# Taps two to a product on half-width tiles, state tiles and loads regrouped, and more of the scan's scaling on ScalarE, in a gated sum of an S5 scan and a long convolution

## The chip, the core and the metric

The kernel runs on one core of one Trainium2 chip. The metric is device time in microseconds (us) of one execution. The engines named below are TensorE (PE in the profile; PEld is its weight load), VectorE (DVE), ScalarE (ACT), GpSimd (POOL) and SyncE (SP). SyncE only hands out transfers (its queue is SPq); GpSimd hands out the transfers that add to their destination.

## What is computed

S = 2048 steps, D = 1024 channels, P = 1024 complex states, all inputs in bf16. The reference, cut:

```python
def A(x, Lambda, B, C, log_dt, Dskip):              # the scan
    Lam_bar = exp(exp(log_dt) * Lambda)
    Bu = x @ (((Lam_bar - 1) / Lambda)[:, None] * B).T
    h[t] = Lam_bar * h[t - 1] + Bu[t]
    return 2 * (h @ C.T).real + x * Dskip
def Bf(q, k, v, shift_k, ssm_k, ssm_D):             # the convolution, q is x
    k_shift[t] = sum(k[t - i] * shift_k[:, i] for i in range(4))    # the four taps
    kv = k_shift * v
    return q * (causal_conv(kv, ssm_k) + kv * ssm_D)
g = sigmoid((x * gate_w).sum(-1, keepdims=True))
out = g * A(...) + (1 - g) * Bf(x, k, v, ...)
```

## The kernel before

**Order.** The instructions of every engine are issued in the order of the program (`put`, line 92; nearly all instructions therefore have line 94 in the profile, and groups are told apart by their tiles). What decides is thus where a step is written, on its own engine's queue and on those of the engines it needs. Generators (`step`, `steps`, `run`, line 948) interleave the parts of longer jobs by hand.

**The convolution** runs over NC = 8 chunks of 128 channels. For a chunk: `load` (line 175) brings k transposed (kT), the filter transposed (kn) and v; `taps` (476) makes the four taps by products with diagonal matrices `dg` (`dgs`, 304); `times_v` (506) multiplies by v and splits into sum and difference (mirror); `fold_K`/`mirror_K` do the same with the filter; `fwd_K` (542) and `fwd_V` (565) transform by products with cosine and sine tables (tiles psk and psv); `products` (578) multiplies the spectra on VectorE; `inverse` (628) transforms back (tile psz) and stores to a scratch in DRAM (cv_scr). The loop from line 1004 is a pipeline: iteration c takes the products of chunk c, the inverse of chunk c-1, the transforms of chunk n = c+1, and the taps and fold of chunk nn = c+2. `tap_sums` (457) has, for each of 16 blocks of 128 steps, four products of a 128 x 128 piece of kT, moved by one step each, with a 128 x 128 diagonal: 64 products of 128 columns a chunk. kT, kn and the v of chunks 0 and 1 share a pool of three rooms (`ld`, 142); v of later chunks comes for two chunks at a time into a tile of the pool of x (`xt_pool`). A `held` load waits for a small write of ScalarE into its tile.

**The scan** has NTB = 4 blocks of 512 steps and NG = 4 groups of 256 states: 16 state tiles in the order of `order` (678), each made in two halves j by products of x and B (`Bu`, 693). Tiles 0 to 3 are made as even and odd steps apart (`Bu_tile`, 717; tiles odd and even), the later ones plain (`Bu_plain`, 743; tile both) and turned afterwards by ScalarE and an adding transfer (`turn_U`). The convolution's loop takes nine of the first twelve halves; three (b0, b1, b2) come after it, at line 1153. `scan` (777) is VectorE's: turn, scan, turn back (hb), and the even steps' share of the odd ones, through two scaled copies q, made by VectorE in scans 0 to 11 and by ScalarE in scans 12 to 14. `turn_C` (1117) scales C's columns: two products by ScalarE, two by VectorE, and a sum, by VectorE or, for 4 and 5, by an adding transfer. `plan` (1223) lists which halves (B), rows (C) and groups of rows (G) of the output products (tile psy) follow each scan.

## Time and profile before

| | us |
|---|---|
| three runs: median, lowest, highest | 399.96, 399.20, 402.22 |
| the profiled execution, and its span | 400.61, 398.8 |
| busy TensorE, VectorE, ScalarE, GpSimd | 386.1, 376.8, 287.4, 72.2 |
| 512 products of the taps, busy | 31.2 |
| 52 scalings q<-hb by VectorE, mean and busy | 0.355, 15.2 |
| 12 scalings Q<-hb by ScalarE, mean and busy | 0.709, 7.7 |
| 6 sums CT<-CT,m by VectorE, mean | 1.226 |

A row of the groups gives the operation, output <- input by the program's names, the number of instructions, busy time (overlaps counted once), the mean duration of one, and the idle time of the engine ahead of them with what ended it. Durations of matmuls include their way through the array, so that a stream of them advances faster than the mean suggests: a stream's time divided by its number is the pace. The chain of waits is the work that ended last, followed back from the end.

### The profile page before, as it was taken

The numbers are of one execution on the slowest core, as the hardware profiler recorded it, in microseconds if no ns is written. First come the engines' busy times: TensorE is split into PE (matmuls) and PEld (weight loads), VectorE is DVE, ScalarE is ACT, GpSimd is POOL, SyncE is SP. The second block draws the span as 40 slices with busy tenths as digits, with TensorE's granted clock in tenths as the row PEclk, the third lists the DMA queues.
The fourth block names the chain that finished last, engine by engine and source line by source line (L and its number), as shares of the span: only waits on it lengthen the run. The fifth ranks groups of instructions, "written<-read, shape, count | busy, mean of one in ns | idle before, by whom it ended". The sixth has DMA issues, their size and how long they took to land.

```text
span 398.8 us, 6544 instructions
## 1 busy us (share of the span) xinstructions
PE 386.1 (97%) x2437; PEld 206.0 (52%) x2437; DVE 376.8 (94%) x610; ACT 287.4 (72%) x434; POOL 72.2 (18%) x96
## 2 busy tenths in 40 slices
PE   8999899999999999999999999979999999999995
PEld 5456357474656647566444444424444444444442
DVE  8799999999999999999999899999999999999944
ACT  4797995969878796765429799936978874996201
POOL 3011030200202011020001010503344233433000
PEclk9999999999999999999999999989999999999999
DMA  7969993996929398097994799978999998988402
GB/s 160 159 142 223 205 261 70 231 213 138 210 58 230 56 156 190 28 156 113 209 204 88 180 196 188 195 164 167 199 188 178 253 261 142 218 163 170 121 0 106
DMA packets 129601, 65.72 MB, mean 165 GB/s; under 512 B 106393, under 2 KB 113313, under 8 KB 129570
## 3 DMA queue, kind: packets, MB, share of 16 engines
q1 hardware_dynamic: 117664, 42.22, 48.7%
q0 software_dynamic: 11824, 23.07, 33.8%
q8 instruction: 19, 0.31, 0.3%
q14 instruction: 12, 0.10, 0.1%
q10 hardware_dynamic: 82, 0.02, 0.0%
HBM read 12.86 MB, written 8.39 MB: 53 GB/s over the span
## 4 chain that ended last, share of the span: by engine, by line
PE 68%; DVE 19%; ACT 6%; issue 4%; DMA 2%; POOL 0%; DVEq 0%; ACTq 0%; POOLq 0%
PE psy L94 27%; PE both L94 12%; PE psk L94 7%; PE taps L94 5%; PE psz L94 4%; DVE BT L94 4%; PE psv L94 3%; PE foldk L94 3%; PE even L94 3%; DVE wkh L94 3%; DVE CT L94 2%; ACT Vh L94 2%; PE odd L94 2%; DVE W L94 2%; DMA ks<-lo 2%
## 5 line engine op out<-in xcount | busy, mean ns | idle before, releaser
L94 PEld LDWEIGHTS <-BT 128*128 128x128 bf16 x640 | 62.2, 98 | 47.8
L94 PE MATMUL both<-xT,BT 128*128 128x512 bf16 x384 | 83.7, 379 | 0.0
L94 PE MATMUL psy<-CT,hb 128*128 128x512 bf16 x256 | 59.4, 387 | 2.3 <-DVE CT L94 2.3
L94 PE MATMUL psy<-CT,U 128*128 128x512 bf16 x256 | 57.4, 379 | 0.0
L94 PEld LDWEIGHTS <-hb 128*128 128x128 bf16 x256 | 25.3, 99 | 33.9 <-issue 5.1
L94 POOL DMA_DIRECT2D U<-Q x24 | 23.3, 983 | 100.8 <-ACT Q L94 61.0
L94 ACT ACTIVATE U<-both 128x512 bf16<-128x512 f32 x48 | 26.4, 593 | 20.4 <-PE both L94 20.1
L94 PEld LDWEIGHTS <-U 128*128 128x128 bf16 x256 | 25.1, 98 | 30.2
L94 ACT ACTIVATE Vh<-psv 128x1024 bf16<-128x1024 f32 x32 | 31.0, 1033 | 11.9 <-PE psv L94 11.9
L94 DVE TENSOR_TENSOR_SCAN W<-rv,init,A 128x256 bf16<-128x256 f32 x48 | 32.2, 730 | 0.0
L94 PE MATMUL taps<-dg,kT 128*128 128x128 bf16 x512 | 31.2, 223 | 0.0
L94 POOL DMA_DIRECT2D G<-wkh x8 | 9.7, 1218 | 115.5 <-DVE wkh L94 115.5
L94 PEld LDWEIGHTS <-kT 128*128 128x128 bf16 x512 | 29.8, 100 | 1.0 <-issue 0.2
L94 PEld LDWEIGHTS <-SF 128*128 128x128 bf16 x184 | 18.0, 98 | 20.0 <-issue 1.5
L94 PE MATMUL psk<-eok,SF 128*128 128x512 bf16 (+1 forms) x120 | 28.1, 354 | 0.0
L94 ACT ACTIVATE Q<-U,lam 128x512 bf16<-128x512 bf16 (+1 forms) x48 | 27.7, 606 | 0.0
L94 PE MATMUL psz<-G,CI 128*128 128x512 bf16 x64 | 24.3, 380 | 2.4 <-DVE G L94 1.9
L94 PE MATMUL psz<-G,SI 128*128 128x512 bf16 x64 | 24.3, 379 | 0.0
L94 DVE TENSOR_TENSOR wkh<-BT,Vh 128x3072 bf16<-128x3072 bf16 (+4 forms) x20 | 21.8, 1111 | 0.0
L94 DVE TENSOR_TENSOR wkh<-Kh,Vh 128x3072 bf16<-128x3072 bf16 (+2 forms) x16 | 21.3, 1350 | 0.0
L94 ACT ACTIVATE BT<-psy,gcols 128x1024 bf16<-128x1024 f32 x5 | 5.4, 1109 | 21.8 <-PE psy L94 21.8
L94 ACT ACTIVATE m<-psy,gcols 128x1024 bf16<-128x1024 f32 x8 | 8.9, 1113 | 16.6 <-PE psy L94 16.6
(189 smaller groups left out, 780.7 us busy)
## 6 DMA issues: line engine op xcount, KB each, us to landing
U<-Q POOLq DMA_DIRECT2D x24, 256.0 KB, 5.3
G<-wkh POOLq DMA_DIRECT2D x6, 768.0 KB, 8.1
cv_scr<-cv SPq DMA_DIRECT2D x16, 256.0 KB, 2.6
v<-in_B_v_dram SPq DMA_DIRECT2D x3, 1024.0 KB, 9.6
out_dram<-m SPq DMA_DIRECT2D x8, 256.0 KB, 5.6
BT<-cv_scr SPq DMA_DIRECT2D x7, 256.0 KB
out_dram<-BT SPq DMA_DIRECT2D x7, 256.0 KB, 2.0
ks<-lo POOLq DMA_DIRECT2D x6, 256.0 KB, 7.4
```

The lines of the kernel that those rows point to most:

```text
L94: i = f(*a, **kw)
```

## The change

- **Taps.** Chunks 2 to 7 use a packed form. `spread` copies kT so that the partitions hold 64 channels twice, the second time moved by two steps: kB for the upper channels and kT itself for the lower ones. A product then makes two taps of 64 channels at once (`packed_sums`), with `dg` tiles of 128 x 64. There are still 64 products a chunk, of 64 columns. `columns` makes the coefficients for this with eight small products and two steps of VectorE.
- **Loads.** kB takes a room of `ld`; v is loaded for chunks 2 and 3 together and then one chunk at a time into halves of one tile. The loads of the next chunk stand right behind the taps, in the order v (held), B or x, kT, kn. The loads of x for block 2 stand at the head of iteration 6.
- **State tiles.** Tiles 0 to 3 are spread in smaller parts over iterations 1 to 6, three halves of tiles 4 and 5 are run in iteration 6, and one after the loop; b10 (the first half of tile 8) moves ahead of the scans, and tile 13 ahead of the first output row, in rooms of its own.
- **Scaling.** Scans 4, 5, 6, 9, 10 and 11 have q made by ScalarE, as 12 to 14 had. C's columns 0 and 1 are summed by adding transfers, and the turning of 6 and 7 stands inside scan 3.

```diff
-            w = 1 if c < 2 else 2
-            if w == 1:
-                t = ld.tile([128, NT, 1, 128], BF16, name="v", tag="ld")
+            w = 2 if c == 2 else 1
+            if c == 2:
+                lds["v2"] = xt_pool.tile([128, NT, 2, 128], BF16, name="v2", tag="xT")
+            if c < 2:
+                t = ld.tile([128, NT, 128], BF16, name="v", tag="ld")
             else:
-                t = xt_pool.tile([128, NT, 2, 128], BF16, name="v2", tag="xT")
-            move(t.rearrange("p n k d -> p n (k d)"),
-                 vf.rearrange("(n p) d -> p n d", p=128)[:, :, c * 128:(c + w) * 128])
+                t = lds["v2"][:, :, c % 2:c % 2 + w].rearrange("p n k d -> p n (k d)")
+            if held:
+                hold(t[:, 0, 0:1])
+            move(t, vf.rearrange("(n p) d -> p n d", p=128)[:, :, c * 128:(c + w) * 128])
             for k in range(w):
-                lds["v", c + k] = t[:, :, k]
+                lds["v", c + k] = t[:, :, k * 128:(k + 1) * 128]
             return
...
             load_t(t[:, PAD:], kf[:, cc])
+            if c >= 2:
+                lds["kB", c] = ld.tile([128, PAD + S], BF16, name="kB", tag="ld")
         lds[which, c] = t
+    def spread(c):
+        a, b = lds["kT", c], lds["kB", c]
+        lo, hi, n = slice(0, 64), slice(64, 128), PAD + S
+        move(b[lo, 8:], a[hi, 8:])
+        move(b[hi, 10:], a[hi, 8:n - 2])
+        yield
+        move(a[hi, 10:], a[lo, 8:n - 2])
     kT0 = ld.tile([128, PAD + S], BF16, name="kT", tag="ld")
-    v0 = ld.tile([128, NT, 1, 128], BF16, name="v", tag="ld")
+    v0 = ld.tile([128, NT, 128], BF16, name="v", tag="ld")
     put("pool", nc.gpsimd.memset, kT0[:, 0:PAD], 0.0)
...
         load_t(kT0[:, PAD + hs.start:PAD + hs.stop], kf[hs, 0:128])
-        move(v0[:, ns, 0], vf.rearrange("(n p) d -> p n d", p=128)[:, ns, 0:128])
-    lds["kT", 0], lds["v", 0] = kT0, v0[:, :, 0]
+        move(v0[:, ns], vf.rearrange("(n p) d -> p n d", p=128)[:, ns, 0:128])
+    lds["kT", 0], lds["v", 0] = kT0, v0
     load("kn", 0)
...
         copy(gwb, psp[:, 1, KS * ND:(KS + 1) * ND])
+        for q in range(4):
+            for t in range(2):
+                mm(psp[t * 64:t * 64 + 64, 1, 64 + q * ND:64 + (q + 1) * ND],
+                   skr[:, q // 2 * 64:q // 2 * 64 + 64, q % 2 + 2 * t], ident[32:32 + ND, 32:32 + ND], True, True)
+        copy(pcol2, psp[:, 1, 64:64 + 4 * ND].rearrange("p (i j) -> p i j", j=ND))
+        tt(ident2, ident[:, 0:64], ident[:, 64:128], ALU.add)
     def dgs(c, on_dve=False):
+        if c >= 2:
+            dg = ks_pool.tile([128, 2, 2, 64], BF16, name="dg2", bufs=1)
+            for q in range(4):
+                if on_dve:
+                    ts(dg[:, q // 2, q % 2], ident2, pcol2[:, q, c:c + 1], None, ALU.mult)
+                else:
+                    act(dg[:, q // 2, q % 2], ident2, func=ACT.Identity, scale=pcol2[:, q, c:c + 1])
+            return dg
         dg = ks_pool.tile([128, KS, 128], BF16, name="dg", bufs=1)
...
+    def packed_sums(halves, dg, h):
+        ps = ps2([128, 8, 128], "taps")
+        for n in range(8):
+            for e, k in enumerate(halves):
+                for m in range(2):
+                    k0 = PAD + (8 * h + n) * 128 - m
+                    mm(ps[:, n, e * 64:e * 64 + 64], k[:, k0:k0 + 128], dg[:, e, m], m == 0, m == 1)
+        return ps
     def of_blocks(ks, h):
...
     def taps(c, dg):
-        kT = lds.pop(("kT", c))
+        kT, kB = lds.pop(("kT", c)), lds.pop(("kB", c), None)
         ks = ks_pool.tile([128, 4, 4, 128], BF16, name="ks")
         for h in range(2):
-            act(of_blocks(ks, h), by_block(tap_sums(kT, dg, h)), func=ACT.Copy)
+            sums = tap_sums(kT, dg, h) if c < 2 else packed_sums((kT, kB), dg, h)
+            act(of_blocks(ks, h), by_block(sums), func=ACT.Copy)
         kss[c] = ks
...
         tb, g = order[i]
+        if i == 13:
+            V_ = s5p["v13"].tile([128, 2, 2, HB], BF16, name="V13")
+            O_ = lam_pool.tile([128, 2, 2, HB + 2], BF16, name="O13", tag="lamd")
+            Us[tb, g] = V_, O_[:, :, :, 2:]
+            turns_U[i] = turn_U(g, V_, O_)
+            return [Bu_plain(tb, g, V_, O_, j) for j in range(2)]
         if i in (10, 11):
...
             else:
-                home = uu[0 if i in (0, 1, 13, 14) else 1] if i < 6 or i in (13, 14) else s5p["uu"]
+                home = uu[0 if i in (0, 1, 14) else 1] if i < 6 or i == 14 else s5p["uu"]
                 U = home.tile(shape, BF16, name="U")
...
                     act(ends[:, tb % 2, g], U[:, 1, :, :, HB - 1], func=ACT.Copy)
-                if halved:
-                    yield
+                yield
         yield
...
     put_off = []
+    scaled_by_act = (4, 5, 6, 9, 10, 11, 12, 13, 14)
...
             tt(hb[:, 1], hb[:, 1], b[:, 0], ALU.add)
-            by_act = tb == NTB - 1 and not last
-            if by_act:
+            by_act = tb * NG + g in scaled_by_act
+            if tb * NG + g == 3:
+                run(turning[7])
+            if by_act and tb == NTB - 1:
                 q = [s5p["Q"].tile([128, 2, 2, HB], BF16, name="Q") for k in range(2)]
...
-    old = ahead = none
-    tiles = (b for i in range(6) for b in Bu(i))
+    old = none
+    parts = (None for i in range(4) for b in Bu(i) for _ in b)
+    tiles = (b for i in (4, 5) for b in Bu(i))
...
         if c == 0:
+            load("kT", 2)
             load("kn", 2)
-            load("kT", 2)
             load("v", 2)
             load_BT(0, 0)
-        if c == 0:
+            run(spread(2))
             p1 = products(0, 1)
...
             step(tv)
+            load("kT", 3)
             load("kn", 3)
-            load("kT", 3)
             load_BT(0, 1)
...
             continue
-        if c == 1:
-            load("v", 4)
+        if c == 6:
+            load_xT(2)
         tabs, back, prod = turn_table(c - 1) if c <= NG else none, inverse(c - 1), products(c)
+        apart = spread(nn) if nn < NC else none
         step(old)
         step(tabs)
+        step(apart)
         step(back)
...
         run(back)
+        run(apart)
         run(old)
-        if c == 2:
-            load("v", 6)
         if nn < NC:
             dg = dgs(nn)
-        bu = next(tiles) if c == 4 else ahead if c == 6 else none
-        step(bu)
+        if c % 2 == 0:
+            step(parts)
         fwd_K(n, (0, 1))
-        step(bu)
+        if c % 2 == 0:
+            step(parts)
         fwd_K(n, (2, 3))
         if c == 6:
-            load_xT(2, held=True)
             run(sp)
...
             taps(nn, dg)
+        if nn + 1 < NC:
+            load("v", nn + 1, True)
+            if c == 1:
+                load_BT(1, 0)
+            elif c in (2, 3):
+                load_xT(1, (3 - c,))
+            load("kT", nn + 1)
+            load("kn", nn + 1)
+            if c == 1:
+                load_BT(1, 1)
         step(prod)
...
             step(tv)
-        bu = [next(tiles) for _ in range({1: 1, 2: 1, 3: 1, 5: 1, 6: 3}.get(c, 0))] + [none, none]
+        if c < 6:
+            steps(parts, 2)
+        else:
+            run(next(tiles))
+        fwd_V(n, (0, 1))
+        if c < 6:
+            step(parts)
+            if c in (1, 3):
+                step(parts)
+        else:
+            run(next(tiles))
+        fwd_V(n, (2, 3))
         if c == 5:
-            bu[1] = ahead = next(tiles)
-        step(bu[0])
-        fwd_V(n, (0, 1))
-        if nn + 1 < NC:
-            load("kn", nn + 1, True)
-            load("kT", nn + 1)
-        if c in (1, 2):
-            load_BT(1, c - 1)
-        elif c in (3, 4):
-            load_xT(1, (c - 3,))
-        step(bu[0])
-        step(bu[1])
-        fwd_V(n, (2, 3))
-        if bu[1] is not ahead:
-            step(bu[1])
-        run(bu[2] if c == 6 else none)
-        if c == 2:
+            step(parts)
+        elif c == 6:
+            run(next(tiles))
+        if c == 1:
             lam_diag(1, lam_pool)
...
     def turn_C(pi):
-        by_sum = pi in (4, 5)
-        if by_sum:
+        by_sum = pi in (0, 1, 4, 5)
+        if pi in (4, 5):
             m = [s5p["Q"].tile([128, D], BF16, name="Q") for c in range(2)]
...
     load_CT(0)
-    load_CT(1)
     load_BT(2, 0)
     load_BT(2, 1)
-    load_CT(2)
     load_BT(3, 0)
     load_BT(3, 1)
+    load_CT(1)
+    load_CT(2)
     load_CT(3)
...
         steps(prod, 3)
-        b0, b1, b2 = tiles
-        run(b0)
+        run(next(tiles))
         run(back)
         gate(1)
-        run(b1)
+        gate(2)
         run(prod)
...
         run(turns_U[6])
-        run(b2)
-        gate(2)
         steps(turning[0], 2)
...
         run(b8)
+        steps(turning[1], 2)
+        run(b9)
+        b10, b11 = Bu(8)
+        run(b10)
         back = inverse(c)
...
         run(back)
-        run(b9)
-        steps(turning[1], 2)
     h3.close()
...
     s5p["io"] = pool("io", 2)
+    s5p["v13"] = pool("v13", 1)
...
     NS = NTB * NG
-    plan = ["B8", "B9 B10", "B11", "B12 C0", "C1", "C2", "C3 B13", "B14 B15", "G10", "G11", "G12 G13", "G20", "G21",
+    plan = ["B8", "B9 B10", "B11", "B12 B13 C0", "C1", "C2", "C3 B14", "B15", "G10", "G11", "G12 G13", "G20", "G21",
             "G22 G23", "", ""]
...
         yield
+        if j == 3:
+            run(turning[6])
...
                 combine(k)
-                if tl == 1 and put_off:
-                    put_off[-1][0]()
+    run(turning[0])
+    run(turning[1])
     step(scans[0])
...
             else:
-                (Bu_next if unit[0] == "B" else Cy_row)(int(unit[1:]))
-        if put_off and j != 13:
+                (Bu_next if unit[0] == "B" else Cy_row)(int(unit[1:]), *([[b11]] if unit == "B8" else []))
+        if put_off:
             put_off[-1][0]()
```

## What I expected

> **What bounds the kernel now.** The profiled run took 400.61 us with a span of 398.8, 1.8 outside it; the median of the three runs, 399.96, is 0.65 lower. I read the page's totals, the chain of waits, the timelines of SyncE and TensorE at the places of the edits, the DMA list, and windows for the clock.
>
> ```profile
> PE 386.1 (97%) x2437; PEld 206.0 (52%) x2437; DVE 376.8 (94%) x610; ACT 287.4 (72%) x434; POOL 72.2 (18%) x96
> ```
>
> TensorE and VectorE are both nearly full, so a saving on one alone is worth little. The chain says who leads where:
>
> ```profile
> 46.48 1.90 PE psz L94 x8
> ...
> 58.73 3.68 PE taps L94 x64
> ...
> 212.03 0.78 PE p L94 x32
> ...
> 311.15 82.92 PE psy L94 x384
> ```
>
> From 31 to 46 it is VectorE, from 46.5 (iteration c=1) to 137 mostly TensorE, from 142 to 172 VectorE (products), to 223 TensorE, to 266 VectorE (first scans, C turned), then TensorE to 394.09. Two more views decide: SyncE's queue and TensorE in c=0.
>
> ```profile
> 24.91 3.72 SPq L94 DMA_TRANSPOSE kT<-in_B_k_dram  x1
> 28.68 0.58 SPq L94 DMA_DIRECT2D v<-in_B_v_dram  x1
> 29.31 6.49 SPq L94 DMA_TRANSPOSE BT<-in_A_B_re_dram  x1
> 35.90 3.56 SPq L94 DMA_TRANSPOSE kn<-in_B_ssm_k_dram  x1
> ```
>
> ```profile
> 32.62 3.74 PE L94 MATMUL taps<-dg,kT 128*128 128x128 bf16 x64
> ...
> 44.76 0.22 PE L94 MATMUL foldk<-rows,refl 1*128 1x128 bf16 x1
> 46.48 0.39 PE L94 MATMUL psz<-G,CI 128*128 128x512 bf16 x1 [1.49 <-DVE G L94]
> ```
>
> SyncE hands over a transpose in about 2 us and is held while the DMA engines are full; chunk 2's taps ran at 32.6, when SyncE was still at BT. TensorE then had 1.5 us of air before 46.48.
>
> **The taps.** Chunks 2 to 7 keep 64 products each, at 64 columns instead of 128. Pairs of weight load and product stream at 6.91/32 = 216 ns for 512 columns, 1.75/16 = 109 for 256, 3.68/64 = 57.5 for 128, and 0.78/32 = 24.4 for the gate's one column. The step per column is about 0.41 ns, so 64 columns should take 31 ns (bounds 24.4 and 57.5). That saves 26.5 x 64 = 1.70 us a chunk: 8.5 us for chunks 3 to 7, whose taps come after 46.48, and 1.7 in c=0, used below.
>
> **The copies.** Each such chunk gets three copies of 256 KB inside the on-chip memory on SyncE's queue; the third waits for the first two, and the taps wait for the third. The nearest rows are other 256 KB moves of that queue.
>
> ```profile
> cv_scr<-cv SPq DMA_DIRECT2D x16, 256.0 KB, 2.6
> out_dram<-BT SPq DMA_DIRECT2D x7, 256.0 KB, 2.0
> ```
>
> In c=0 the copies stand behind BT, whose handing over ends at 35.8. The first two go out at 35.9 and 36.5, behind 512 KB of BT and beside a gather: at the 290 GB/s that the DMA view shows there, BT lasts to 38, the pair to about 40.5. The third is issued then and lands 2.0 to 2.6 later: 43 (41.5 to 45). Taps(2) waits from 32.5 to 43, and behind it on TensorE stand the rest of K's transform, V's and the fold: 36.20 to 44.98, 8.8 us. Then 43 + 2.0 + 8.8 = 53.8 in place of 46.48, +7.3. VectorE waits too: chunk 1's products need that V. The clock adds to it; elsewhere it fell after waits of 1.28 and 1.03 us:
>
> ```profile
> 266.00:268.00 2.00, 1.77 (x5) 0.56 0.02 6
> 268.00:270.00 2.00, 2.00 (x7) 0.59 0.00 0
> ```
>
> That is 4 us at 0.57, 1.7 us lost; the 1.5 us wait at 46.48 lost none. I take 0.9, so **+8.2** (5.8 to 11). The Trainium skill ("TensorE: Matmul & The Clock Gate", Part 1) has the clock halve after an idle window of about 3.4 us. By that rule all 1.7 would be paid, the sum 0.8 higher; the trace agrees on the drop (0.56), not on the idle time it takes.
>
> In c=1 the queue is kT 3 and kn 3 (both waiting for taps(2), whose room they take), BT, two of xT, then the copies: five transposes of 2 to 2.7 us from 46.4 on, a pair at about 58, the third landing near 65.5. TensorE needs 12.2 us from psz (46.48) to taps (58.73), so it arrives at 66.9: 1.5 us of air. In c=2 to 4 two transposes fewer leave about 4. Behind SyncE's wait for the pair stand cv's second store and v; a store later by 2 us still precedes the next use of its buffer. I charge **+0.7** (0 to 20, see rivals). The extra 0.79 MB a chunk meets a DMA share of 0.70 to 0.86 there; the gathers into G have over 10 us until used.
>
> **State tiles.** Two more of 16 products, about 3.46 us each, run before c=7, and after the first psy row (C0) two fewer remain (U13 is ahead of it): +6.9 ahead, -6.9 behind. From c=1 to c=4 TensorE has 92.8 us now (four times 15.6 + 3.7 of taps + 3.9 of tile) and 93.7 then, VectorE some 22.7 each: TensorE still leads. In c=5 and c=6 VectorE leads (products, 22.5 us each, and the overlap), and new waits at psz(5) and V of chunk 7 come to 3.1 us against 2.2 now: **+0.9**. xT 2 must land before tile 4: v's room is free when VectorE is done with chunk 7's v, 9 us ahead of it; no cost, 2 us if late.
>
> **C turned by gather; q by ScalarE.** On VectorE two sums of 1.23 us go (C 0 and 1), with them its wait of 1.5 us for m, and the turning of 6 and 7 moves ahead of scan 3's q and U (2.5 us). So VectorE, 8.1 late at chunk 5's products, ends C 7 at 266.1 + 8.1 - 2.3 - 1.5 - 2.5 = 267.9. TensorE reaches C0 at 257.56 + 8.2 - 8.5 + 6.9 + 0.9 = 265.1 and its last group at 270.3, after it. What C0 loses now goes:
>
> ```profile
> 264.18 1.02 PE L94 MATMUL psy<-CT,hb 128*128 128x512 bf16 x4 [1.28 <-DVE CT L94]
> 266.23 9.60 PE L94 MATMUL psy<-CT,hb 128*128 128x512 bf16 x36 [1.03 <-DVE CT L94]
> ```
>
> Arriving at 257.56, its 6.9 us would end at 264.5; it ended, with the lower clock, at 268.9: **-4.4** (0 to -4.4). Six scans' q: 24 x 0.285 = 6.8 us leave VectorE after C0, where TensorE leads: worth nothing by itself, cover for the rest. ScalarE gets 24 x 0.62 = 15 us there, 79 busy of the 104 us from 266 to 370 becoming 94. Eight small products and two VectorE steps at the start cost **+0.4** (0 to 0.8). The holds on ScalarE are 0.2 us each, behind evictions TensorE has finished; v by chunk moves the same bytes.
>
> Sum: +0.4 + 8.2 - 8.5 + 0.7 + 0.9 - 4.4 = **-2.7 us**, so 397.9 on the profiled run's scale, 397 on the median's. With the bounds of these terms, 392 to 401.
>
> **Rivals.**
> - The copies of chunk 2 cost nothing: they pass BT on the DMA engines, or land in time some other way. For: 0.53 MB is 2 us of transfer. Against: the queue's order, and a handing over that ends at 35.8. It gives 8.2 less: 389.
> - The copies are late in every chunk, the case on the slower side: two hops, each in full DMA traffic beside the gathers.
>
> ```profile
> ks<-lo POOLq DMA_DIRECT2D x6, 256.0 KB, 7.4
> ```
>
>   At 5.5 us a hop instead of 2.6 the third lands 5.8 late, less air of 1.5 in c=1 and 4 in the three others: 4.3 + 3 x 1.8 = 9.7, so 407. It decides from 5.2 us a hop on. For: the row above, and v's 9.6 us for 1 MB. Against: that row is an accumulating gather on another queue, while plain moves show 2.0 to 2.6.
> - The weight load, not the columns, sets a product's pace: each stays at 57.5 ns and 8.5 + 1.7 come back, 407. Against it, the gate loads 128x128 weights for every column at 24.4 ns. The Trainium skill (same page, "LDWEIGHTS") times a load by its 128 columns at 107 ns whatever follows, which speaks for this rival; the 24.4 ns of the trace does not agree with that as a pace.
> - ScalarE, 90% full after C0, delays evictions. For: every q waits for its scan in ScalarE's queue ahead of psy's evictions. Against: four product buffers cover 20 us of rows. Some 3 us: 400.
>
> **How the numbers follow.** 1% is 4 us, about what a measurement of this kernel can tell from no change. Forecast 42%, 397 with its own range 392 to 401, some 15 of the 42 below 396; free copies 25% (389); late copies 18% (407); weight pace 5% (407); ScalarE 10% (400). Faster by over 1%: 15 + 25 = 40%. Within: 27 + 10 = 37%. Slower: 23%. The range 388 to 405 takes in the forecast, the free copies, ScalarE and the near end of the late copies, and leaves out about 2 in 10.
>
> **What would show it.** Taps on dg2 near 2.0 us for 64; more says weights. TensorE idle before chunk 2's taps from 32.5 to about 43 with the third copy as releaser, psz at 54 to 55 instead of 46.48; a psz near 47 says free copies. Waits for kT before the taps of chunks 3 to 7 under 2 us; several of 2 or more say late copies. C0 without a wait for C, and 0.56 gone from the clock there. ScalarE waited for by psy would say the fourth rival. If VectorE leads in c=1 to c=4, my count of TensorE there is wrong.

## The result and the profile after

The changed kernel takes 432.71 us (median of four runs, 429.15 to 434.01); the kernel before took 399.88 beside it. The ratio is 1.080 with an interval of 1.072 to 1.088: 8% slower, where 397 us and a range up to 405 were forecast. The profiled execution is the fastest of the four, 429.15 us with a span of 427.3; positions below are its own. The ratios below are to the kernel before, run beside each kernel; they leave out executions more than 1.5% slower than the fastest of their kernel, so that a ratio can differ from the quotient of two medians.

The page of the changed kernel: busy time of each engine, the granted clock by slices, and the chain's shares by line.

```profile
PE 378.3 (89%) x2411; PEld 200.8 (47%) x2445; DVE 367.2 (86%) x586; ACT 300.8 (70%) x456; POOL 76.0 (18%) x100
...
PEclk9996699799998998999999999999999999999998
...
PE psy L94 22%; SPq L94 10%; DMA kT<-kT 8%; DMA kB<-kT 6%; PE both L94 4%; PE taps L94 4%; ACT Q L94 3%; PE psv L94 3%; DVE BT L94 3%; ACT Vh L94 3%; PE odd L94 3%; DVE wkh L94 2%; DMA ks<-lo 2%; PE even L94 2%; ACT m L94 2%
```

TensorE and VectorE are each less busy by 8 to 10 us, and both have lost their full span: 89% and 86% where 97% and 94% stood. They wait. ScalarE has 13 us more to do and GpSimd 4, neither near full by the page. New on the chain are the two hops of the copies, 14% of the span, and SyncE's queue (SPq), 10%; and the clock has dips in the first two fifths, where it had none. TensorE's waits say the same (total, times, longest):

```profile
PE taps L94 <- DMA kT<-kT: 28.1, 5, 11.9
PE psy L94 <- ACT U L94: 5.0, 2, 3.4
```

The chain of waits in order of time (start, length, what) shows the hops one behind the other, here of c=0, c=1 and c=2:

```profile
36.76 5.59 DMA kB<-kT
...
42.41 2.87 DMA kT<-kT
...
45.33 3.60 PE taps L94 x64
...
62.47 9.64 DMA kB<-kT
...
72.17 5.14 DMA kT<-kT
...
...
93.75 4.25 DMA kB<-kT
...
98.07 7.68 DMA kT<-kT
```

In c=3 they took 4.40 and 7.68 us. Where the wait was long the taps then ran at half the clock. Windows around the taps alone (start:end, length, TensorE's busy time and products, VectorE, ScalarE, granted clock, DMA share, GB/s), the first after a wait of 11.92 us, the second after one of 1.64:

```profile
45.30:49.00 3.70, 3.60 (x64) 0.00 (x0) 1.06 (x2) 0.50 0.00 0
...
105.80:107.90 2.10, 2.06 (x64) 0.00 (x0) 0.93 (x1) 1.00 0.67 120
```

The second is the narrow product at full clock: 2.06/64 = 32 ns, against 57.5 of before.

### The profile page after: what moved, and what is told of

The parts are those of the page before. It is cut to its first block, busy times and chain, and to the rows that moved or that the text cites. A ratio compares the mean times of both kernels' runs of the same rounds, so it can differ in the third digit from the quotient of the medians.

```text
span 427.3 us, 6555 instructions
## 1 busy us (share of the span) xinstructions
PE 378.3 (89%) x2411; PEld 200.8 (47%) x2445; DVE 367.2 (86%) x586; ACT 300.8 (70%) x456; POOL 76.0 (18%) x100
## 4 chain that ended last, share of the span: by engine, by line
PE 41%; DMA 18%; ACT 17%; SPq 10%; DVE 9%; issue 4%; ACTq 0%; DVEq 0%
PE psy L94 22%; SPq L94 10%; DMA kT<-kT 8%; DMA kB<-kT 6%; PE both L94 4%; PE taps L94 4%; ACT Q L94 3%; PE psv L94 3%; DVE BT L94 3%; ACT Vh L94 3%; PE odd L94 3%; DVE wkh L94 2%; DMA ks<-lo 2%; PE even L94 2%; ACT m L94 2%
## 5 line engine op out<-in xcount | busy, mean ns | idle before, releaser
L94 PE MATMUL psy<-CT,hb 128*128 128x512 bf16 x251 | 57.3, 379 | 5.3 <-ACT U L94 5.0
L94 PE MATMUL psy<-CT,U 128*128 128x512 bf16 x236 | 53.4, 379 | 0.2
L94 PE MATMUL taps<-dg,kT 128*128 128x64 bf16 (+1 forms) x320 | 25.1, 222 | 29.6 <-DMA kT<-kT 28.1
L94 ACT ACTIVATE Vh<-psv 128x1024 bf16<-128x1024 f32 x32 | 31.0, 1034 | 11.5 <-PE psv L94 11.4
L94 POOL DMA_DIRECT2D U<-Q x22 | 21.5, 993 | 92.1 <-ACT Q L94 58.8
L94 ACT ACTIVATE ks<-taps 128x1024 bf16<-128x1024 f32 x14 | 14.0, 1025 | 33.1 <-PE taps L94 33.1
L94 PEld LDWEIGHTS <-kT 128*128 128x128 bf16 x320 | 22.4, 110 | 31.0 <-DMA kT<-kT 23.2
L94 ACT ACTIVATE U<-both 128x512 bf16<-128x512 f32 x44 | 24.1, 594 | 15.7 <-PE both L94 15.4
L94 DVE TENSOR_TENSOR U<-U,q 128x512 bf16<-128x512 bf16 (+2 forms) x42 | 19.2, 484 | 8.7 <-ACT q L94 8.1
L94 ACT ACTIVATE Q<-U,lam 128x512 bf16<-128x512 bf16 (+1 forms) x44 | 25.4, 606 | 0.0
L94 DVE TENSOR_TENSOR G<-BT,Vh 128x4096 bf16<-128x4096 bf16 (+1 forms) x5 | 9.3, 1862 | 15.2 <-ACT Vh L94 15.2
```

Of the source, the lines that this page charges most:

```text
L94: i = f(*a, **kw)
```

## The experiments

The milestones below are read from TensorE's timeline: the starts of psz(0) to psz(6), of row C0, and the end of the last product, in us. psz(c) opens iteration c+1, so what c=1 costs lies between psz(0) and psz(1). The two last rows are the first two experiments.

| | psz(0) | psz(1) | psz(2) | psz(3) | psz(4) | psz(5) | psz(6) | C0 | end |
|---|---|---|---|---|---|---|---|---|---|
| before | 46.48 | 69.63 | 93.21 | 117.19 | 140.35 | 164.41 | 193.80 | 257.56 | 394.1 |
| after | 57.87 | 89.73 | 115.09 | 144.42 | 172.56 | 196.43 | 226.32 | 293.95 | 422.8 |
| no copies | 47.13 | 72.02 | 95.64 | 119.13 | 142.97 | 166.84 | 198.10 | 264.15 | 393.0 |
| full taps, no copies | 47.25 | 72.15 | 97.48 | 122.60 | 148.13 | 172.00 | 203.23 | 269.00 | 399.5 |

The theory to test: the third copy comes late, two hops behind each chunk's load, and with the lower clock behind that wait it is the whole loss of the convolution; ScalarE's added q is a second loss, behind it.

**What the copies cost.**

```diff
...
-                lds["kB", c] = ld.tile([128, PAD + S], BF16, name="kB", tag="ld")
+                kB = ld.tile([128, PAD + S], BF16, name="kB", tag="ld")
+                put("pool", nc.gpsimd.memset, kB[:, 0:PAD], 0.0)
...
-            sums = tap_sums(kT, dg, h) if c < 2 else packed_sums((kT, kB), dg, h)
+            sums = tap_sums(kT, dg, h) if c < 2 else packed_sums((kT, kT), dg, h)
...
-            run(spread(2))
...
-        apart = spread(nn) if nn < NC else none
...
-        step(apart)
...
-        run(apart)
```

> The changed kernel without the three copies of each chunk: kB is allocated as before but only its first 16 columns are set, and the packed taps of chunks 2 to 7 read kT for both halves, so the sums of those six chunks are not K's taps. All else is the changed kernel's. Theory 1 (the whole loss of the convolution is the wait for the third copy and the lower clock behind it): taps(2) starts near 32.5 us, no wait of TensorE ahead of taps over 2 us in any chunk, psz(6) at 185 to 191 us instead of 226, median 391 to 399 us. Rival 1 (the added bytes and v's 256-byte rows hold up the gathers, and VectorE with them): only the copies' share of 4.7 of 5.8 MB goes, v's small rows stay, 400 to 410. Rival 2 (the new order of loads, state tiles and products loses the time): over 420.

399.83 us, ratio to before 1.0037 (1.0003 to 1.0071). Without the copies all 33 us of the loss are gone. Of the rivals, the order of loads and tiles is out, and v's small rows cost little, if anything. By differences of the table's rows the copies cost 10.7 us in c=0, 7.0 in c=1, 1.7 in c=2, 5.8 in c=3, 4.3 in c=4 and nothing more in c=5: 29.6. But psz(6) came at 198, not at 185 to 191: without the copies, and so without K's true taps, the kernel only draws level with before. Its TensorE waits:

```profile
PE psz L94 <- DVE G L94: 5.0, 2, 3.0
PE psy L94 <- ACT U L94: 3.4, 1, 3.4
```

VectorE's G is now what psz waits for in the convolution, and U's evictions by ScalarE are what psy waits for behind it.

**What the narrow taps bring.** The same with before's four full-width products in every chunk (`sums = tap_sums(kT, dg, h)`, and dgs as before).

> The changed kernel with before's four full-width products a tap block in all eight chunks, no copies and kB only touched (the output is the reference's again). Against the run without copies this tells what the narrower products are worth by themselves. Theory 1: 57.5 instead of 31 ns for each of 64 products in six chunks, 10.2 us where TensorE leads throughout: psz(6) 7 to 10 us later than without copies, median 399 to 408. Rival (VectorE leads the convolution once the copies are gone): under 3 us between the two runs.

406.26 us, ratio 1.0167 (1.0133 to 1.0201). Against the run without copies, 6.4 us of the median and 5.1 at psz(6), where 10.2 were counted. By the rows of the table the saving arrives whole in c=2, c=3 and c=4 (1.7, 1.6 and 1.7 us) and not at all in c=0, c=1 and c=5. At psz(0) the shorter taps turn into a longer wait for VectorE's G (TensorE's timeline, first without copies, then with full taps):

```profile
47.13 0.45 PE L94 MATMUL psz<-G,CI 128*128 128x512 bf16 x1 [2.98 <-DVE G L94]
```

```profile
47.25 0.39 PE L94 MATMUL psz<-G,CI 128*128 128x512 bf16 x1 [1.34 <-DVE G L94]
```

From 48 to 50 us the granted clock was 0.50 behind the longer wait and 1.00 behind the shorter, which takes c=1's saving too; at psz(5) the wait for G is 1.98 us instead of 0.27. The row "full taps" against "before" also prices the tiles and the start: +9.4 at psz(6), where 0.4 + 6.9 + 0.9 = 8.2 were forecast.

**q on ScalarE.**

```diff
-    scaled_by_act = (4, 5, 6, 9, 10, 11, 12, 13, 14)
+    scaled_by_act = (12, 13, 14)
```

> The changed kernel with the q of scans 4, 5, 6, 9, 10 and 11 back on VectorE (only scans 12, 13 and 14 on ScalarE, as before). Theory 2 (ScalarE, full from 278 on, holds up the evictions of psy by about 7.5 us): psz(6) unchanged at 226, the stretch from C0's end to the last product shorter by 5 to 8 us, ScalarE under 95% busy there, median 424 to 428. Rival (the stretch is TensorE's own, or VectorE takes the time with the 6.8 us that come back): 431 to 437.

426.73 us, ratio 1.0694 (1.0623 to 1.0764): below the changed kernel by 6.0 us in the medians and by 4 in the ratios, whose intervals overlap. The traces price it more closely: from C0's start to the end it took 125.4 us, against 128.8 with the q on ScalarE. The first of the added q runs at 309 us, behind C0, so what the two runs differ by ahead of C0 is not the q's. The windows ahead of G10 show who was full, first with nine scans on ScalarE (after), then with three (columns: TensorE, its weight loads, VectorE, ScalarE, GpSimd, clock, DMA share, GB/s):

```profile
320.00:341.00 21.00, 17.92 (x110) 8.52 (x111) 19.73 (x45) 20.94 (x37) 7.33 (x9) 1.00 0.84 161
```

```profile
320.00:341.00 21.00, 20.84 (x123) 9.90 (x125) 20.65 (x48) 18.12 (x33) 8.78 (x10) 1.00 0.94 180
```

20.94 of 21 us: the q stand in ScalarE's queue ahead of U's evictions, and TensorE waits for a product buffer (its timeline in the changed kernel). With three scans on ScalarE it has no such wait there, so the wait is the whole difference:

```profile
341.47 1.89 PE L94 MATMUL psy<-CT,hb 128*128 128x512 bf16 x8 [3.39 <-ACT U L94]
```

**q on ScalarE in the order of before.**

```diff
-            by_act = tb == NTB - 1 and not last
-            if by_act:
+            by_act = tb * NG + g in (4, 5, 6, 9, 10, 11, 12, 13, 14)
+            if by_act and tb == NTB - 1:
...
-                if tl == 1 and put_off:
-                    put_off[-1][0]()
...
-        if put_off and j != 13:
+        if put_off:
```

> The kernel before with only the six more scans' q put on ScalarE. Theory 2: ScalarE gets 15 us more after C0 and TensorE waits for evictions of psy there, 403 to 408. Rival (it only shows in the changed order of tiles and rows, or four product buffers cover it): 398 to 401.

398.90 us, ratio 0.9996 (0.9976 to 1.0015): nothing. The same 15 us on ScalarE are free here: TensorE waits for no eviction behind C0. It has two more state tiles (6.9 us) to do there before it reaches G10. Behind C0 the two edits are thus harmless one by one, the tiles in the run ahead of this and the q in this one. That the tiles which the change took away were the cover of the q which it added fits the four kernels; no run moved the tiles alone.

**The bytes without the wait.** All copies are made, but the third writes kB once more and the taps read kT alone:

```diff
-        move(a[hi, 10:], a[lo, 8:n - 2])
+        move(b[hi, 10:], a[lo, 8:n - 2])
...
-            sums = tap_sums(kT, dg, h) if c < 2 else packed_sums((kT, kB), dg, h)
+            sums = tap_sums(kT, dg, h) if c < 2 else packed_sums((kT, kT), dg, h)
```

> The changed kernel with all three copies of a chunk moved as before, in two hops on SyncE's queue (the third writes kB once more, behind the second, so kT's upper half is not overwritten), but nobody reads them: the packed taps take kT for both halves, so the sums of chunks 2 to 7 are not K's taps. This has the copies' bytes and SyncE's wait for the pair, without TensorE's wait. Theory 1 (TensorE's wait is the loss): within 4 us of the run without copies, median 398 to 404, psz(6) at 198 to 202. Rival 1 (the bytes and the blocked queue hold up gathers and stores): 410 or more, with the G gather's landing back near 9.3 us.

413.89 us, ratio 1.0374 (1.0344 to 1.0405): the rival's number, but not its place. From psz(1) to psz(5) it took 95.2 us against 94.8 without copies, so from c=2 to c=5 bytes and SyncE's wait cost nothing. Of the 15.1 us by which its last product is later, 11.4 come in c=1, and show in SyncE's lines for xT, first this run's, then those without copies:

```profile
52.35 16.13 SPq L94 DMA_TRANSPOSE xT<-in_A_x_dram  x2
```

```profile
46.14 4.97 SPq L94 DMA_TRANSPOSE xT<-in_A_x_dram  x2
```

SyncE took up chunk 3's kT at 45.4 instead of 36.9, behind chunk 2's copies; xT came 6 us later, and so fell among the accumulating gathers that go out from 52.5 to 56 in both runs. TensorE waited 9.9 us for it. Between psz(6) and C0 another 5.3 us were lost, 3.3 of them in a wait for a later xT; c=6 gave 2.0 back.

**The clock.**

```diff
+            warm = {2: 185, 3: 110, 5: 65, 6: 30}.get(c, 0) if h == 0 else 0
...
+        for _ in range(warm):
+            mm(ps[:, 0], ident, ident, True, True)
```

> The changed kernel with idle products (ident by ident, into the buffer that the taps fill next) ahead of the taps of chunks 2, 3, 5 and 6: 185, 110, 65 and 30 of them at 57.5 ns, a little less than TensorE's waits of 11.9, 7.3, 4.7 and 2.6 us there. The waits for the third copy stay; what goes is the lower clock behind them. Theory 1's second part (taps of 3.4 instead of 2.07 us and more slow products behind them, some 1.6 us a chunk in four chunks): granted clock 1.0 in the taps, psz(6) 5 to 7 us earlier, median 425 to 428. Rival (the slow clock lies under VectorE's or SyncE's own chain and costs nothing): 431 to 434.

425.16 us, ratio 1.0676 (1.0643 to 1.0709), some 5 us below the changed kernel by the ratios, whose intervals just part. The lower clock is a real part of the loss, by this figure about a seventh, but its size is uncertain (the medians are 7.6 us apart, the profiled executions 1.8). Chunk 2's was not even saved, as its idle products ended 3.0 us early (timeline of TensorE):

```profile
33.50 10.49 PE L94 MATMUL taps<-ident 128*128 128x128 bf16 x185
47.02 0.23 PE L94 MATMUL taps<-dg,kT 128*128 128x64 bf16 x2 [3.03 <-DMA kT<-kT]
...
47.41 0.22 PE L94 MATMUL taps<-dg,kT 128*128 128x64 bf16 x2
...
47.54 0.29 PE L94 MATMUL taps<-dg,kT 128*128 128x64 bf16 x2
```

**Fewer hops, by transposes of 64 channels.** First two of them and one hop, then four and none:

```diff
...
+                for e, u in enumerate((t, lds["kB", c])):
+                    load_t(u[0:64, PAD:], kf[:, c * 128 + e * 64:c * 128 + e * 64 + 64])
...
+        for t in (lds["kT", c], lds["kB", c]):
+            move(t[hi, 10:], t[lo, 8:n - 2])
```

> The changed kernel with K's chunk loaded by two transposes of 64 channels, each into the lower half of one of the two tiles, so that two copies (lower half to upper half of each tile) are all that is left and none waits for another copy. The reference's output again. Theory 1 (two hops in a row in a closed loop from one chunk's taps over the loads and copies to the next chunk's taps, 26 to 32 us round where before took 23.5): the second hop of 2.9 to 9.4 us leaves the loop, taps wait for a few us in c=0 and c=1 and little later, psz(6) 203 to 212, median 405 to 415. Rival 3 (a transpose of 64 channels holds SyncE as long as one of 128, and what the hop saved goes to the longer queue): psz(6) over 218, median 423 or more.

> The changed kernel with no copies at all: four transposes of 64 channels fill the four halves straight from the input, the shifted ones two columns further. The reference's output. Theory 1: no hop behind the load; at 2.0 to 2.5 us of SyncE each, four transposes and kn take 12.5 us of SyncE in a round of 23.5, so the taps wait only in c=0 (until about 40 us) and median is 402 to 410. Rival 3 (these transposes cost SyncE or the DMA engines twice what a whole one does, 1.0 MB a chunk): taps wait in every chunk, 420 or more.

2406.61 us and 4355.24 us. Nothing is learned of the hops, but much of the load: over 64 channels it is no longer a transposing transfer (DMA list: output <- input, queue, kind, count, size, time to landing):

```profile
kT<-in_B_k_dram SPq DMA_DIRECT2D x6, 256.0 KB, 175.7
kB<-in_B_k_dram SPq DMA_DIRECT2D x6, 256.0 KB, 333.9
```

It goes element by element, (1695842 - 134306) / 12 = 130,000 packets each for 64 x 2048 elements, and the second lands behind the first: (2406.61 - 400) / 12 = 167 us for half a chunk, where a whole one lands in 4.8 in the run without copies.

**Fewer hops, by loading K twice.** Both tiles get the whole chunk by a transpose of 128 channels; a copy in each then makes the shifted half, and neither waits for the other.

```diff
...
+                b = lds["kB", c] = ld.tile([128, PAD + S], BF16, name="kB", tag="ld")
...
+                load_t(b[:, PAD:], kf[:, cc])
...
         move(a[hi, 10:], a[lo, 8:n - 2])
+        move(b[lo, 10:], b[hi, 8:n - 2])
...
```

> The changed kernel with K's chunk transposed twice over all 128 channels, once into kT and once into kB; one copy in each tile (lower to upper half in kT, upper to lower in kB, with the two tap pairs of kB's products swapped to match) then makes the shifted half, so no copy waits for a copy. Order of the queue as in the change. The reference's output. Theory 1 (a closed loop from one chunk's taps over loads and two hops to the next chunk's taps): a hop of 2.9 to 9.4 us leaves the loop, a transpose of 2.0 to 2.6 us enters it, 3 to 6 us a chunk less where it bound: psz(6) 206 to 216, median 411 to 421. Rival 3 (the second transpose costs what the hop did): 428 or more.

429.99 us, ratio 1.0759 (1.0711 to 1.0808): almost nothing gained. From c=2 on it is as expected in part (psz(1) to psz(5) 100.3 us instead of 106.7 after), but in c=0 and c=1 the longer queue gives it back: the copies go out at 39.1 instead of 36.2 and at 74.7 instead of 61.9.

**The copies ahead of everything else.** The same, with v, BT and xT behind each chunk's copies.

```diff
...
+            load("kT", nn + 1)
+            load("kn", nn + 1)
+            run(spread(nn + 1))
             load("v", nn + 1, True)
...
```

> The run with two loads, and SyncE's queue in another order: for each chunk the two transposes of K and kn first, the copies right behind them, and only then v, BT and xT. Theory 1: the loop from taps to taps is three transposes and one hop, 12 to 15 us, shorter than TensorE's 23.5; only chunk 2 is left with a wait of 3 to 6 us, median 404 to 410, within 10 of the run without copies. Rival 1 (what stands behind the copies, xT above all, is late in its place, as in the run of unread copies, where TensorE waited 9.9 us for xT): 412 or more.

440.40 us, ratio 1.0936 (1.0867 to 1.1006), the slowest of the orders tried. The waits for copies are down to 4.7 us, all in chunk 2, as the loop theory has it; the time went to what stood behind them. TensorE's waits, and a window of c=1:

```profile
PE odd L94 <- DMA xT<-in_A_x_dram: 21.9, 1, 21.9
...
PE taps L94 <- DMA kT<-kT: 3.7, 1, 3.7
...
PE taps L94 <- DMA kB<-kB: 1.1, 1, 1.1
```

```profile
60.00:65.00 5.00, 5.00 (x55) 2.69 (x54) 5.00 (x6) 5.00 (x6) 1.02 (x3) 1.00 1.34 34
```

The two transposes of xT, at 60.4, share the DMA engines with the gathers issued from 56 to 61. The engines are full (share 1.34) and move 34 GB/s; SyncE is held for 25.5 us.

**The early order with q on VectorE, and the same from chunk 3 on.**

> The early order with q of scans 4, 5, 6, 9, 10 and 11 back on VectorE. The 6 us that this gave in the changed kernel lie behind the convolution, so they add: 398 to 404 (6 less than the early order). Rival (what is gained in one place is taken back in the other): within 2 us of the early order.

> The early order with q on VectorE and chunk 2's taps full width as before, so packed taps only from chunk 3 on, and the loads of chunk 3 need not wait for chunk 2's taps. Theory 1: no wait for a copy is left in any chunk; against the run without copies 6 us less for q and 1 to 2 us more for chunk 2's wider products: 394 to 398, faster than the kernel before by 0.3 to 1.3 percent. Rival (VectorE and the state tiles bind the convolution by then): 398 to 402, no gain on the kernel before.

429.12 us (416.06 to 431.48, too wide for an interval) and 416.51 us, ratio 1.0402 (1.0352 to 1.0451). In the second no wait for a copy is left, and TensorE waits 19.3 us for xT instead, in c=1 and c=4. The copies' theory is right about the copies and says nothing of where the total goes.

**Copies by GpSimd.** No transfer is added; GpSimd copies between the halves.

```diff
-        move(b[lo, 8:], a[hi, 8:])
+        put("pool", nc.gpsimd.tensor_copy, b[lo, 8:], a[hi, 8:])
...
```

> The changed kernel with each chunk's three copies made by GpSimd (64 partitions to the other 64, all three in a row at the place where the pair stood) instead of transfers on SyncE's queue. The reference's output. A copy of 64 x 2064 has no row in the traces; from GpSimd's 0.60 us for setting 128x256 it is at most 4.8 us, and at least 1.1 (VectorE's 0.285 us for 512 columns). Theory 1 (SyncE's queue and the DMA beside the gathers make the copies late): 3.3 to 14.5 us on an engine that is 12 percent busy there, no transfer is moved, median 400 to 410. Rival 4 (the making itself, or GpSimd's gathers held behind it, costs as much): 415 or more.

> Copies by GpSimd and the q of scans 4, 5, 6, 9, 10 and 11 back on VectorE: 5 to 7 us below the run with copies by GpSimd, 394 to 404.

> As the last, with chunk 2's taps at full width and no copies for it. If chunk 2's copies are still late (its taps are due at 33.5 us, kT lands near 30), this is 2 to 6 us faster than the last; if they are in time, 1 to 2 us slower (64 products of 57.5 instead of 31 ns). 394 to 400; the kernel before stands at 399.

429.11, 422.91 and 424.26 us, ratios 1.0771 (1.0683 to 1.0859), 1.0595 (1.0508 to 1.0682) and 1.0624 (1.0559 to 1.0688). Chunk 2's taps still wait 3.7 us in the first two, until GpSimd's third copy and VectorE's dg beside it are done; no later taps wait. In the first, psz waits 15.9 us for VectorE's G. VectorE has the same 586 instructions there and is busy for 396.8 us instead of the 367.0 without copies. Two of its groups (count | busy, mean ns), with GpSimd's copies and then without copies:

```profile
L94 DVE TENSOR_TENSOR wkh<-Kh,Vh 128x3072 bf16<-128x3072 bf16 x8 | 17.4, 2173 | 0.0
L94 DVE TENSOR_TENSOR A<-A,trn 128x512 bf16<-128x512 bf16 x30 | 11.3, 419 | 0.2
```

```profile
L94 DVE TENSOR_TENSOR wkh<-Kh,Vh 128x3072 bf16<-128x3072 bf16 x8 | 14.0, 1751 | 0.0
L94 DVE TENSOR_TENSOR A<-A,trn 128x512 bf16<-128x512 bf16 x30 | 11.3, 419 | 0.2
```

The first is an operation of the convolution, where GpSimd copies; the second, of the scans, where it doesn't, is unchanged to the nanosecond. Chunk 2's share can't be told apart: 1.0595 and 1.0624 overlap.

**Copies by ScalarE**, two a chunk with K loaded twice, from chunk 3 on, q on VectorE, and the first iteration's BT and xT ahead of K.

```diff
...
+        act(a[hi, 10:], a[lo, 8:n - 2], func=ACT.Copy)
+        act(b[lo, 10:], b[hi, 8:n - 2], func=ACT.Copy)
...
```

> The changed kernel with K transposed twice (kT, kB), one copy in each made by ScalarE just ahead of the taps' weights, packed taps from chunk 3 on, BT and xT of the first iteration ahead of K's, and the q of scans 4, 5, 6, 9, 10, 11 on VectorE. Two copies of 64 x 2054 cost ScalarE 4.5 us a chunk (1.14 us for 128x1024 in its rows) on top of 20.0 busy of 23.6 us in the run without copies: 0.9 a chunk over, 394 plus 2 to 6: 396 to 401. Rival 1 (transposes and gathers collide again and xT or ks is late): 405 or more.

411.16 us, ratio 1.0291 (1.0244 to 1.0337): the best with packed taps and real copies, and still 3% over before. How its excess is shared between ScalarE and the transfers stays open.

**C turned by gather, in the kernel before.** First with C 0 and 1 finished ahead of the first scan, as in the change, then at their old place; 6 and 7 are turned where the change turns them.

```diff
-        by_sum = pi in (4, 5)
+        by_sum = pi in (0, 1, 4, 5)
...
+    run(turning[0])
+    run(turning[1])
     step(scans[0])
```

> The kernel before with only this part of the change: C 0 and 1 turned by a gather instead of a VectorE sum, finished ahead of the first scan, C 7 turned inside scan 3 and C 6 between its halves. The prediction's term: TensorE's two waits for CT at C0 (2.3 us) and the low clock behind them go, -4.4 us (0 to -4.4): 394.6 to 397, ratio 0.989 to 0.995. Rival: VectorE only passes the wait on to the first scans' hb and U, which feed the same rows, ratio over 0.997.

> As the run with C turned by a gather, but C 0 and 1 are finished behind the first scan, where the kernel before finishes them (in the last run VectorE idled 9.5 us for ScalarE's m ahead of the first scan). VectorE loses 1.23 to 2.46 us of sums ahead of C0, C 7 is done some 3.8 us earlier than before's 266.1, at about 262.3, and TensorE wants it at 262.8. The prediction's term holds: no wait over 0.5 us for CT at C0, the granted clock stays at 1.0, 394.1 to 396.5, ratio 0.989 to 0.994. Rival: the gathers of C 4 and 5 land too late (3.9 us waited in the last run) or hb of scan 3, now behind C 6, is waited for: ratio 0.996 or more.

404.73 us, ratio 1.0145 (1.0116 to 1.0174), and 403.83 us, ratio 1.0123 (1.0101 to 1.0145): slower both times. In the first VectorE idled 9.5 us ahead of the first scan, for ScalarE's m. In the second, three views tell why (DMA list, ScalarE's and TensorE's timeline):

```profile
CT<-m POOLq DMA_DIRECT2D x4, 256.0 KB, 13.6
```

```profile
244.68 2.19 ACT L94 ACTIVATE m<-CT,mc2i 128x1024 bf16<-128x1024 bf16 x2 [6.18 <-DMA CT<-m]
```

```profile
251.81 15.55 PE L94 MATMUL both<-xT,BT 128*128 128x512 bf16 x64 [8.61 <-ACT U L94]
```

A gather reads m until it lands, 13.6 us after its issue; there are two buffers of m, so ScalarE waits to write the next, with U's evictions behind it, and TensorE waits for those. The VectorE sum that was saved took 1.23 us and freed m at once. In the changed kernel VectorE waits 1.84 us for m, once (before: 1.50), the gathers land in 5.0 us, and C0 does not wait for C. It waits for an eviction of U instead (timeline of TensorE):

```profile
293.95 6.42 PE L94 MATMUL psy<-CT,hb 128*128 128x512 bf16 x29 [1.56 <-ACT U L94]
```

## Why the prediction was wrong

| step, as the prediction had it | forecast | measured |
|---|---|---|
| narrow taps, 31 ns a product | 31 ns | 32 ns (2.06 us for 64) |
| what they bring, chunks 2 to 7 | 10.2 us (8.5, and 1.7 used inside the next row) | 5.1 at psz(6), 6.4 in the median |
| copies of chunk 2, with the clock | +8.2 (5.8 to 11) | +10.7 |
| copies late in c=1 to c=4 | +0.7 (0 to 20) | +18.8 |
| start, state tiles and their waits, to psz(6) | +8.2 | +9.4 |
| psz(6) to C0 | 0 | +3.9, of which 3.5 are two waits for evictions of U |
| C0's wait for C gone, two tiles fewer behind C0 | -11.3 (-4.4 and -6.9) | -11.1 (with q on VectorE: 125.4 against 136.5) |
| q on ScalarE | 0 | +3.4 |

In the profiled executions the measured rows add up: -5.1 + 10.7 + 18.8 - 1.4 (c=6 shortens the delay) + 9.4 + 3.9 - 11.1 + 3.4 = 28.6, where the ends, 394.1 and 422.8, are 28.7 apart.

The step that failed is the price of a hop. It was read from the fastest rows of the same queue and the same size, cv_scr 2.6 us and out_dram<-BT 2.0. The DMA list of before has other plain moves of 256 KB on that queue, all slower, with medians from 4.1 to 8.6 us; three of them:

```profile
out_dram<-m SPq DMA_DIRECT2D x8, 256.0 KB, 5.6
...
xr<-in_A_x_dram SPq DMA_DIRECT2D x6, 256.0 KB, 5.2
...
xlast<-in_A_x_dram SPq DMA_DIRECT2D x4, 256.0 KB, 7.3
```

So "plain moves show 2.0 to 2.6" was not what that list says. Behind the two rows chosen stand five landings, after 1.99 to 2.97 us, and each of the five was handed over while no accumulating gather was under way; the three landings behind out_dram<-m, after 4.2 to 7.0 us, all had one. The hops of c=0 to c=4 part along the same line: the four that were handed over with no gather under way took 2.9 to 4.4 us, the six that went into a running one took 5.1 to 9.6. In c=1 the gather of G went out 1.1 us ahead of the pair (timeline of GpSimd) and landed at 71.99, the pair at 72.11:

```profile
61.35 1.20 POOL L94 DMA_DIRECT2D G<-wkh  x1 [12.31 <-DVE wkh L94]
```

In the run that loads K twice, the copies of c=1 went out at 74.7, just as the last gather landed, and the first of them took 3.5 us. No run moved a hop or a gather alone, so that the gathers are the cause is what these rows show together, not a test of it.

In c=1 the two hops took 9.6 and 5.1 us, in c=2 4.3 and 7.7, in c=3 4.4 and 7.7. With those the rival's own sum comes near: (9.6 + 5.1 - 5.2) - 1.5 of air = 8.0 for 7.0 measured, and (4.3 + 7.7 - 5.2) - 4 = 2.8 in c=2 and c=3, for 1.7 and 5.8, the second with the lower clock. The rival "copies late in every chunk" was right in mechanism, place and threshold (5.2 us a hop; 6.0 to 7.4 came), and had 18% because the row that was nearest in place, ks<-lo at 7.4, was set aside for its form. For c=1 to c=4 it counted 9.7 us, where 18.8 came, since a hop took more than 5.5 us and the clock fell: the prediction charged the lower clock once, in c=0, and the trace has it in four chunks. What its 407 lacks besides it shares with the forecast: chunk 2, the taps and ScalarE. By the rule of the Trainium skill ("TensorE: Matmul & The Clock Gate", Part 1) that the prediction quotes, an idle window of about 3.4 us halving the clock, the waits of 11.9, 7.3 and 4.7 us all pay; the trace agrees (0.50, 0.58 and 0.59 over the taps behind them), and shows 0.59 after 2.6 us too.

In c=0 the mechanism was right to the microsecond in its first part (copies out at 36.2, 35.9 forecast). The pair then landed at 42.4 instead of 40.5: the 290 GB/s that it was priced at are those of the microsecond from 36 to 37 (291), while from 36 to 39.5 the view has 239. The third took 2.9 instead of 2.5: 45.3, just over the upper bound of 45. Here only sizes were off.

The ScalarE rival came true as well, and at its size, 3.4 us for "some 3", against the argument that four product buffers cover it. The cover had been counted in rows of psy; what TensorE waits for is U's eviction ahead of them. The two tiles fewer were priced as a gain only, while by the runs of q they look to have been ScalarE's slack too.

Two terms held: behind C0 the wait for C and the two tiles gave 11.1 us of the 11.3 forecast, and a narrow product took 32 ns. That each chunk's 1.7 us would arrive in five chunks behind 46.48 did not hold; they arrived in three. That VectorE's wait for m would go did not hold either.

The free-copies rival at 389 could not have come either: without copies the kernel takes 399.8. The taps bring 4 to 5 us less, because VectorE's G is next behind TensorE in the convolution, the q on ScalarE take 3.4, the stretch from psz(6) to C0 is 2.3 longer, and tiles and start cost 1.2 more. No version here beats the kernel before; the nearest are before with q alone (0.9996) and the change without its copies (1.0037), which does not compute K's taps.

## What to carry to other kernels

Price a moved or added transfer by what will run beside it in its own stage, not by the fastest rows of its queue and size: the hops took 2.9 to 4.4 us with no accumulating gather under way and 5.1 to 9.6 with one, and the error is paid once for every hop in a row. Before counting on a saving in a kernel whose engines are nearly all full, look for the resource that the new step needs: here the DMA engines, SyncE's order, GpSimd and ScalarE were each tried for the same copies, and each charged its own neighbour. Two edits that are free alone can be dear together, as the q and the tiles were, when one removes the work that hides the other.

## What the hardware showed that was not expected

A DMA transpose over 64 instead of 128 channels falls out of its form: 130,000 packets and 167 us for half the bytes of a transfer that lands in 4.8. The Trainium skill ("DMA: Bandwidth & Descriptors", "DMA Transpose (X-bar)", Constraints) has such a fallback with inefficient descriptors for inputs with a free dimension under 128; the trace agrees, and puts the price at some 70 times for a byte.

A GpSimd copy holds VectorE. In one run of copies from 82.9 to 93.9 us, three VectorE operations took 3.45, 3.98 and 2.38 us, where the kernel without copies has 1.75, 2.29 and 0.68: each 1.7 longer, whatever its size. The copies stretched too, to 3.66, 3.33 and 3.84 us, where the shortest of the run took 1.89. The Trainium skill ("SBUF — State Buffer", Terms) calls the port pair of the two engines exclusive, held for a whole instruction; a fixed delay for each operation, near the length of one copy, agrees with that.

The clock fell 3.5 us after TensorE went idle even though it was working again by then: idle from 43.99 to 47.02, two-product steps of 0.06 us until 47.47, then of 0.11. Single waits of 1.1, 1.6 and 2.1 us left it at 1.00.

Transposes that meet accumulating gathers crawl. The two of xT in the first iterations held SyncE for 4.8 to 7.0 us in thirteen kernels (before, after and eleven others; the two with loads of 64 channels are left aside) that had handed them over before the first gather of c=1, or within about 0.5 us of it, and for 10.5, 10.6, 16.1, 17.1 and 25.5 us in the five where the gather was issued earlier than that; the same order of transfers gave once 10.5 and once 25.5. Which of the two holds the other up was not tried.
